# Where C's rows are folded, when a bias bank is seeded and when a doubled product is evacuated: one change to a gated state-space and MLP kernel on one core

## The chip, the core and the metric

The kernel runs on one core of a Trainium2 chip. The core has a matrix engine (TensorE, "PE" in the profile; its weight loads are "PEld"), a vector engine (VectorE, "DVE"), an activation engine (ScalarE, "ACT"), a general engine (GpSimd, "POOL") and a queue engine (SyncE, "SP"). Each takes its instructions strictly in the order in which the program wrote them, and waits on semaphores for what another engine has to finish first. SBUF is the working memory; PSUM, in eight banks, takes what PE computes. The metric is the device time of one launch in microseconds (us), as the median of several runs.

## What is computed

The input x is 2048 rows of 640 columns. Two branches are computed from it and mixed by a gate per row. Cut to what matters:

```python
g = sigmoid((x * gate_w).sum(-1))
# branch A: a diagonal complex state space, 640 states
Lam_bar = exp(exp(log_dt) * Lam)
Bu = x @ (((Lam_bar - 1) / Lam)[:, None] * Bmat).T
h_t = Lam_bar * h_{t-1} + Bu_t                       # over the 2048 rows
a = 2 * real(h @ Cmat.T) + x * Dskip
# branch B: an MLP, 640 -> 1728 -> 640
b = gelu_tanh(x @ w1 + b1) @ w2 + b2
out = g * a + (1 - g) * b
```

## The kernel before

The 2048 rows go through in four chunks of 512 (`c` = 0 to 3), and every chunk through four kinds of stage. The order of the stages is written out by hand at the end of the kernel (L911 to L951), chunk against chunk, so that one chunk's matmuls cover another's vector work.

- **State stage**, `ssm(c)` (L601). For each of five groups of 128 states (`ks`), PE makes x times B, real and imaginary, in two banks of ten matmuls in all (L610). ACT copies each bank out as `bu` (L613). DVE then turns the sequence into a real first-order recurrence, runs two scans (L556) and turns it back into `hs`: for each group `wa`, `wb`, `v`, two scans, `wa`, `wb`, `hs`. That takes DVE far longer than PE takes for the matmuls, so the chains of a chunk run on under the stages that follow. Between chunks the last column of the scan is carried by four small ACT instructions (L564).
- **GELU stage**, `ff1(c)` (L340). Thirteen banks (`kf` = 0 to 12) of five matmuls each (L300); ACT evacuates each by one GELU with its bias (L309). What is left over of the 1728 columns, 64 of them and the gate's one, is `last_tile` (L321): 20 small matmuls into a bank that ACT has seeded with the bias beforehand (`last_bank`, L317), with a GELU (L327) and a tanh for the gate (L329) behind them. In a dictionary `at` the stage is handed further work to issue ahead of a given `kf`.
- **Second MLP product**, `fin_b(c)` (L697). A two-by-two block product by seven multiplications instead of eight. Each multiplication is 2 times 7 matmuls of 320 columns (L708). Three of its names matter here. `X` is a pair of banks that collects several products; a `fork` (L720) is an ACT copy of that pair, halfway, into a new pair (`Y` or `Z`) on which other products are added. `Q` is the doubled product: it is needed in both column halves, so ACT evacuates it, scaled by the gate, into `gq` (`part_7`, L741), and a GpSimd DMA that adds on arrival (`twice`, `plus`, L653) brings it into both halves of a row tile. In chunks 0 to 2 the target of that DMA is the output's own tile `gb`; in chunk 3 (`gs` given) it is a tile of `GS`, two of which lie in the unused parts of `xA` and `w1c_lo`, and DVE adds them to `gb` later (L829).
- **Product with C**, `fin_a(c)` (L769): ten matmuls of 320 columns for each half of a row tile, on banks that ACT has seeded with x times Dskip (`seed`, L644); DVE adds gate and `gb` and the rows go out (L787). The last chunk has `fin_s` (L832) in its place, again by seven multiplications (L843, with DVE's evacuations at L860 and L872).

Before C can be used it has to be multiplied by complex factors: **`fold(ks)`** (L506). For each of the five groups of rows ACT writes two products into two f32 buffers `t1` and `t2` (L508 and L510, both in what is `xA`, free in that time), and DVE adds two more to them and writes C in place (L514, once for `CT_re`, once for `CT_im`). There is one `t1` and one `t2`. So the first DVE instruction of a fold waits for both ACT instructions (the second of them reads the old `CT_re`), and the ACT instructions of the next fold wait for the DVE instructions of this one. All five folds have to be through before `fin_a(0)`.

What sets the order on DVE is a planner with clocks of its own (L220 to L251). The pieces of a scan chain are put into a list with `later`. `dve_now(ready, cost, fn)` first lets out every piece of the list that could start ahead of `ready` on the planner's clock, and then issues `fn`. So the place of a fold on DVE is set by the planner's clock for ACT at the time that the fold is issued, while its place on ACT is simply where it stands in the program. `settle` lets out the carries in the same manner.

The PSUM banks go round: a tile that needs one gets the one that was given back first, in the order of the instructions that first write the tiles. On PE the stages around the change come in this order: `ff1(1)`, `ssm(1)`, `fin_b(0)`, `ff1(2)`, `fin_a(0)`; and at the end `fin_a(2)`, `fin_b(3)`, `fin_s(3)`.

Of the kernel before, what the change touches and what calls it, by code (L numbers as in the profile page):

```python
# [24 lines left out]
KF = (F + P - 1) // P  # L25
# [3 lines left out]
H = TPC // 2  # L29
# [13 lines left out]
def kernel(  # L43
# [32 lines left out]
    def bank(dtype=F32):  # L76
        return ps.tile([P, CH * 4 // (4 if dtype == F32 else 2)], dtype, name="bank")
# [153 lines left out]
    def let_out(until, chunk=-1):  # L231
        while pend:
            ready, cost, fn, _ = pend[0]
            start = max(ck.dve, ready)
            if start >= until and not any(x[3] == chunk for x in pend if chunk >= 0):
                return
            pend.pop(0)
            fn()
            ck.dve = start + cost

    def dve_now(ready, cost, fn):
        let_out(ready)
        fn()
        ck.dve = max(ck.dve, ready) + cost
# [4 lines left out]
    def act(cost):  # L249
        ck.act = max(ck.act, ck.pe + 0.2) + cost  # L250
        return ck.act  # L251
# [45 lines left out]
    def ff1_mm(p, c, kf, kd, t0=0, t1=CH, first=None, last=KD - 1):  # L297
        w, f0 = (w1a, 0) if kf < FA else (w1b, FA) if kf < FB else (w1c, FB)
        w = w[kd][:, (kf - f0) * P:(kf - f0 + 1) * P]
        nc.tensor.matmul(p[:, t0:t1], lhsT=w, rhs=xT[c][:, kd, t0:t1],  # L300
                         start=(kd == 0) if first is None else first, stop=(kd == last), skip_group_check=first is not None)
        pe(t1 - t0)

    def ff1_act(p, c, kf):
        s = kf if kf < FA else kf + 1 if kf < 2 * FA else FA
        for p0, p1 in ((0, RE), (RE, P)) if s == FA else ((0, P),):
            dst = eL[p0:p1, :] if p0 else gel[c][p0:p1, :, s, :]
            src = p[p0:p1, :] if p0 else p[p0:p1, :].rearrange("p (i t) -> p i t", i=2)
            nc.scalar.activation(out=dst, in_=src, func=ACT.Gelu_apprx_tanh, bias=b1_c[p0:p1, kf:kf + 1])  # L309
            act(0.69)  # L310
# [3 lines left out]
    def last_bank(c):  # L314
        p = bank()
        pv = p[:, 0:TPC * NL].rearrange("p (a n) -> p a n", a=TPC)
        nc.scalar.activation(out=pv, in_=b1x[:].rearrange("p (o n) -> p o n", o=1).to_broadcast([P, TPC, NL]), func=ACT.Identity)  # L317
        act(0.4)
        return p, pv
# [20 lines left out]
    def ff1(c, k0=0, at={}):  # L340
        for kf in range(k0, KF - 1):
            if kf in at:
                at[kf]()
            p = bank()
            if kf == KF - 3:
                last = last_bank(c)
            for kd in range(KD):
                ff1_mm(p, c, kf, kd)
            ff1_act(p, c, kf)
            let_out(ck.pe)  # L350
            if c > 0:
                settle()
        last_tile(c, *last)
        let_out(ck.pe)
# [151 lines left out]
    def fold(ks):  # L506
        t1, t2 = ft[:, 0, :], ft[:, 1, :]
        nc.scalar.activation(out=t1, in_=CT_im[:, ks, :], func=ACT.Identity, scale=n2im[:, ks:ks + 1])  # L508
        act(0.82)
        nc.scalar.activation(out=t2, in_=CT_re[:, ks, :], func=ACT.Identity, scale=n2im[:, ks:ks + 1])  # L510
        ready = act(0.82)

        def f(CT, sc, t):
            nc.vector.scalar_tensor_tensor(out=CT[:, ks, :], in0=CT[:, ks, :], scalar=sc[:, ks:ks + 1], in1=t,  # L514
                                           op0=ALU.mult, op1=ALU.add)

        dve_now(ready, 0.8, lambda: f(CT_re, c2re, t1))
        dve_now(ready, 0.8, lambda: f(CT_im, n2re, t2))
# [82 lines left out]
    def ssm(c, at={}):  # L601
        hs[c] = hsp.tile([P, 2, 2, KS, HT], BF16, name="hs")
        for ks in range(KS):
            if ks in at:
                at[ks]()
            bu = work.tile([P, 2, CH], BF16, name="bu", bufs=8)
            for ri, BT in enumerate((BT_re, BT_im)):
                p = bank()
                for kd in range(KD):
                    nc.tensor.matmul(p[:], lhsT=BT[ks >= KSA][:, kd, (ks % KSA if ks < KSA else ks - KSA) * P:][:, 0:P], rhs=xT[c][:, kd, :],  # L610
                                     start=(kd == 0), stop=(kd == KD - 1))
                    pe(CH)
                nc.scalar.activation(out=bu[:, ri, :], in_=p[:], func=ACT.Identity)  # L613
                act(0.6)
            scan_ops(c, ks, bu, ck.act)
            let_out(ck.pe)
            settle()
# [22 lines left out]
    def seed(ti):  # L640
        seeded[ti] = []
        for d0, d1 in cuts(ti):
            p = bank()
            nc.scalar.activation(out=p[:, 0:d1 - d0], in_=xn[ti][:, d0:d1], func=ACT.Identity)  # L644
            act(0.45)
            seeded[ti].append(p)
        if ti % TPC < TPC - 2:
            skip(ti + 2)
        if ti + TPC < NT - H:
            load_xn(ti + TPC)  # L650
# [43 lines left out]
    def twice(dst, src):  # L694
        plus(dst.rearrange("p (h d) -> p h d", h=2), src[:].rearrange("p (o d) -> p o d", o=1).to_broadcast([P, 2, HD]))

    def fin_b(c, at={}, gs=None):  # L697
        (a, b), (s1, d) = blocks(c)
        W = lambda h, k: w2_sb[:, h, k * KH:(k + 1) * KH, :]
        quad = [{} for _ in range(H)]  # L700
        gq = [None] * H

        def product(j, name, lhs, rhs, fresh):
            if name not in quad[j]:
                quad[j][name] = bank()
            p = quad[j][name]
            for s in range(KH):
                nc.tensor.matmul(p[:, 0:HD], lhsT=lhs[:, s, j * P:(j + 1) * P], rhs=rhs[:, s, :],  # L708
                                 start=fresh and s == 0, stop=s == KH - 1, skip_group_check=True)
                pe(HD)  # L710
            let_out(ck.pe)

        def both(name, lhs, rhs, fresh=False):
            for j in range(H):
                product(j, name, lhs, rhs, fresh)

        def fork(src, dst):
            for j in range(H):
                quad[j][dst] = bank()
                nc.scalar.activation(out=quad[j][dst][:, 0:HD], in_=quad[j][src][:, 0:HD], func=ACT.Identity)  # L720
                act(0.45)

        def out_of(name, half, h):
            for j in range(H):
                ti = c * TPC + half * H + j
                if gbs[ti] is None:
                    gbs[ti] = fwork.tile([P, D], F32, name="gb")
                nc.scalar.activation(out=gbs[ti][:, h * HD:(h + 1) * HD], in_=quad[j][name][:, 0:HD], func=ACT.Identity,  # L728
                                     scale=gcol[:, 1, ti:ti + 1])
                act(0.47)  # L730

        def hook(i):
            settle()
            if i in at:
                at[i]()

        def part_7():
            for j in range(H):
                ti = c * TPC + H + j
                gq[j] = fwork.tile([P, HD], F32, name="gq", bufs=2)  # L740
                nc.scalar.activation(out=gq[j][:], in_=quad[j]["Q"][:, 0:HD], func=ACT.Identity, scale=gcol[:, 2, ti:ti + 1])  # L741
                act(0.53)

        hook(0)
        both("X", a, W(0, 0), True)
        fork("X", "Y")
        both("Y", b, W(0, 1))
        out_of("Y", 0, 0)
        plus(flat(b), flat(N2[:]))
        hook(1)  # L750
        both("Q", N3, W(1, 0), True)
        both("X", N2, TB)
        fork("X", "Z")
        part_7()
        for j in range(H if gs else 0):
            twice(gs[H + j], gq[j])
        both("X", s1, TA)
        out_of("X", 1, 1)
        hook(2)
        both("Z", d, TC)  # L760
        out_of("Z", 1, 0)
        for j in range(0 if gs else H):
            twice(gbs[c * TPC + H + j][:], gq[j])
        hook(3)
        both("X", b, W(1, 1))
        out_of("X", 0, 1)
        settle()
# [133 lines left out]
    def skips(c, a=0):  # L901
        skip(c * TPC + a)
        skip(c * TPC + a + 1)
# [11 lines left out]
               5: lambda: (w_minus(1), w_plus(B12, TB)),  # L915
               9: lambda: (first_sums(), w_plus(TB, TA), w_plus(TC, TB))})
    gates(0)
    ssm(1)
    gates(1)
    load_xT(2)  # L920
    load_skip()
    fin_b(0, {1: lambda: fold(0), 2: lambda: fold(1), 3: lambda: fold(2)})
    gel_tile(2)
    ff1(2, 0, {1: lambda: fold(3), 4: lambda: fold(4), 7: lambda: skips(0), 9: lambda: seed(0), 11: lambda: seed(1)})
    gates(2)
    fin_a(0, sums(1))
    load_xT(3)
# [54 lines left out]
```

## Time and profile before

| | |
|---|---|
| median of 3 runs | 211.88 us (211.61 to 211.9) |
| the profiled execution | 211.5 us, of which the profiled span is 209.7 us |
| PE busy | 202.4 us, 97% of the span |
| DVE busy | 187.7 us, 89% |
| ACT busy | 147.1 us, 70% |
| POOL busy | 52.1 us, 25% |
| TensorE clock granted | 1.00 throughout |

Every instruction of the profile has a start and a duration in microseconds from the span's start, the engine, the line of the kernel, what it writes and reads, and in square brackets the idle time of its engine just ahead of it with the instruction that ended it. A group is marked by a count (x5). Matmuls are pipelined: the profile gives a single one of 512 columns 0.38 us, but they follow one another every 0.216 us (five start at 79.66, the next five at 80.74 us), and those of 320 columns every 0.136 us (five start at 86.50, the next five at 87.18 us). Short instructions of one kind follow one another on ACT sooner than the sum of their durations too, since the next begins before the last has fully ended.

Where the stages of interest lie on PE (from the timeline):

| stage | PE, from to |
|---|---|
| `ff1(1)` | 30.4 to 45.8 us |
| `ssm(1)` | 45.8 to 56.6 us |
| `fin_b(0)` | 56.6 to 69.9 us |
| `ff1(2)` | 69.9 to 86.5 us |
| `fin_a(0)` to `fin_a(2)` | 86.5 to 182.0 us |
| `fin_b(3)` | 182.0 to 195.3 us |
| `fin_s(3)` | 195.3 to 206.4 us |

### The profile page before, as it was taken

The numbers are of one execution on the slowest core, as the hardware profiler recorded it, in microseconds if no ns is written. First come the engines' busy times: TensorE is split into PE (matmuls) and PEld (weight loads), VectorE is DVE, ScalarE is ACT, GpSimd is POOL, SyncE is SP. The second block draws the span as 40 slices with busy tenths as digits, with TensorE's granted clock in tenths as the row PEclk, the third lists the DMA queues.
The fourth block names the chain that finished last, engine by engine and source line by source line (L and its number), as shares of the span: only waits on it lengthen the run. The fifth ranks groups of instructions, "written<-read, shape, count | busy, mean of one in ns | idle before, by whom it ended". The sixth has DMA issues, their size and how long they took to land.

```text
span 209.7 us, 3618 instructions
## 1 busy us (share of the span) xinstructions
PE 202.4 (97%) x1311; PEld 120.9 (58%) x1311; DVE 187.7 (89%) x308; ACT 147.1 (70%) x293; POOL 52.1 (25%) x83
## 2 busy tenths in 40 slices
PE   8999999989999997999999999999999999999982
PEld 5745444444577543576457777544447777777761
DVE  2589999999998899599999999999999999999583
ACT  3699989996768799991764895367987593058600
POOL 8344077314310500031001044100412045014000
PEclk9999999999999999999999999999999999999999
DMA  6999799999998330259933389920586969945403
GB/s 187 243 220 218 152 299 240 217 210 171 155 173 177 63 65 0 63 102 237 193 81 56 67 144 204 255 84 0 68 175 115 148 166 189 226 114 92 80 16 109
DMA packets 45126, 30.28 MB, mean 144 GB/s; under 512 B 26834, under 2 KB 42548, under 8 KB 45108
## 3 DMA queue, kind: packets, MB, share of 16 engines
q0 software_dynamic: 6448, 12.53, 35.3%
q1 hardware_dynamic: 38084, 17.03, 34.3%
q10 hardware_dynamic: 576, 0.49, 0.7%
q8 instruction: 10, 0.16, 0.3%
q14 instruction: 8, 0.07, 0.1%
HBM read 7.79 MB, written 2.62 MB: 50 GB/s over the span
## 4 chain that ended last, share of the span: by engine, by line
PE 74%; ACT 12%; DVE 6%; issue 3%; DMA 3%; POOL 0%; DVEq 0%
PE bank L610 21%; PE bank L708 18%; PE bank L782 16%; PE bank L300 15%; ACT gel L309 5%; DMA w1c_lo<-gq 3%; PE bank L324 1%; PE bank L259 1%; PE bank L843 1%; DVE ot L860 1%; DVE g L556 1%; ACT xA L508 1%; ACT TB L658 1%; DVE gb L872 1%; ACT xA L510 1%
## 5 line engine op out<-in xcount | busy, mean ns | idle before, releaser
L556 DVE TENSOR_TENSOR_SCAN g<-r_c,carry,v 128x512 bf16<-128x512 f32 x30 | 37.2, 1271 | 0.8
L613 ACT ACTIVATE bu<-bank 128x512 bf16<-128x512 f32 x40 | 23.2, 595 | 20.4 <-PE bank L610 20.4
L309 ACT ACTIVATE gel<-bank,colB 128x512 bf16<-128x512 f32 (+1 forms) x52 | 32.6, 696 | 1.6 <-PE bank L300 1.5
L708 PEld LDWEIGHTS <-gel 128*128 128x128 bf16 x280 | 27.3, 98 | 10.9
L782 PEld LDWEIGHTS <-hs 128*128 128x128 bf16 x240 | 23.4, 98 | 9.0
L708 PE MATMUL bank<-w_sb,gel 128*128 128x320 bf16 x168 | 24.1, 299 | 0.0
L300 PEld LDWEIGHTS <-w1a_sb 128*128 128x128 bf16 x162 | 14.2, 100 | 11.9
L782 PE MATMUL bank<-CT_re,hs 128*128 128x320 bf16 x120 | 20.2, 299 | 0.0
L782 PE MATMUL bank<-CT_im,hs 128*128 128x320 bf16 x120 | 20.2, 299 | 0.0
L728 ACT ACTIVATE gb<-bank,gcol 128x320 f32<-128x320 f32 x32 | 16.0, 525 | 5.4 <-PE bank L708 5.2
L720 ACT ACTIVATE bank<-bank 128x320 f32<-128x320 f32 x16 | 6.8, 424 | 17.1 <-PE bank L708 17.1
L610 PEld LDWEIGHTS <-BT_im 128*128 128x128 bf16 x100 | 9.8, 98 | 11.8
L610 PEld LDWEIGHTS <-BT_re 128*128 128x128 bf16 x100 | 9.6, 98 | 11.0
L534 DVE TENSOR_TENSOR v<-wa,wb 128x1024 bf16<-128x1024 bf16 (+1 forms) x25 | 14.2, 585 | 0.6
L534 DVE TENSOR_TENSOR wa<-TCOS,bu 128x1024 bf16<-128x1024 bf16 x20 | 13.7, 687 | 0.6
L300 PE MATMUL bank<-xA,w1a_sb 128*128 128x128 bf16 (+2 forms) x102 | 14.2, 296 | 0.0
L534 DVE TENSOR_TENSOR wa<-TCOS,g 128x1024 bf16<-128x1024 bf16 x20 | 13.8, 689 | 0.4
L534 DVE TENSOR_TENSOR wb<-TSIN,g 128x1024 bf16<-128x1024 bf16 x20 | 13.7, 684 | 0.0
L534 DVE TENSOR_TENSOR wb<-TSIN,bu 128x1024 bf16<-128x1024 bf16 x20 | 13.7, 684 | 0.0
L708 PEld LDWEIGHTS <-N 128*128 128x128 bf16 x112 | 11.0, 98 | 4.3
L300 PE MATMUL bank<-xB,w1a_sb 128*128 128x512 bf16 x60 | 13.3, 379 | 0.0
L300 PEld LDWEIGHTS <-w1b_sb 128*128 128x128 bf16 x80 | 7.8, 98 | 9.4
(182 smaller groups left out, 389.6 us busy)
## 6 DMA issues: line engine op xcount, KB each, us to landing
out_dram<-ot SPq DMA_DIRECT2D x15, 160.0 KB, 3.9
w_sb<-in_B_w_dram SPq DMA_DIRECT2D x4, 480.0 KB, 6.6
gb<-gq POOLq DMA_DIRECT2D x6, 320.0 KB, 5.2
gel<-N POOLq DMA_DIRECT2D x4, 448.0 KB, 5.4
xn<-in_A_x_dram SPq DMA_DIRECT2D x10, 160.0 KB, 3.4
N<-gel POOLq DMA_DIRECT2D x3, 448.0 KB, 4.5
gel<-gel POOLq DMA_DIRECT2D x3, 448.0 KB, 7.0
N<-N POOLq DMA_DIRECT2D x3, 448.0 KB, 7.9
```

The source lines that it names most:

```text
L259: nc.tensor.matmul(pA[:, 0:n], lhsT=ones(P), rhs=ones(n), start=True, stop=True)
L300: nc.tensor.matmul(p[:, t0:t1], lhsT=w, rhs=xT[c][:, kd, t0:t1], start=(kd == 0) if first is None else first, stop=(kd == last), skip_grou ...
L309: nc.scalar.activation(out=dst, in_=src, func=ACT.Gelu_apprx_tanh, bias=b1_c[p0:p1, kf:kf + 1])
L324: nc.tensor.matmul(p[:, a * NL:(a + 1) * NL], lhsT=xT[c][:, kd, a * P:(a + 1) * P], rhs=w1c[kd][:, n1c - NL:n1c], start=False, stop=(kd == ...
L534: nc.vector.tensor_tensor(out=o, in0=a, in1=b, op=op)
L556: nc.vector.tensor_tensor_scan(s["g"][:, ri, :], r_c[:, ks:ks + 1].to_broadcast([P, CH]), s["v"][:, ri, :], init, ALU.mult, ALU.add)
L610: nc.tensor.matmul(p[:], lhsT=BT[ks >= KSA][:, kd, (ks % KSA if ks < KSA else ks - KSA) * P:][:, 0:P], rhs=xT[c][:, kd, :], start=(kd == 0 ...
L613: nc.scalar.activation(out=bu[:, ri, :], in_=p[:], func=ACT.Identity)
L708: nc.tensor.matmul(p[:, 0:HD], lhsT=lhs[:, s, j * P:(j + 1) * P], rhs=rhs[:, s, :], start=fresh and s == 0, stop=s == KH - 1, skip_group_c ...
L720: nc.scalar.activation(out=quad[j][dst][:, 0:HD], in_=quad[j][src][:, 0:HD], func=ACT.Identity)
L728: nc.scalar.activation(out=gbs[ti][:, h * HD:(h + 1) * HD], in_=quad[j][name][:, 0:HD], func=ACT.Identity, scale=gcol[:, 1, ti:ti + 1])
L782: nc.tensor.matmul(p[:, 0:d1 - d0], lhsT=hs[c][:, a // H, j // KS, j % KS, (a % H) * P:][:, 0:P], rhs=CT[:, j % KS, d0:d1], start=False, s ...
```

## The change

Three edits. The first moves `last_bank` from ahead of the GELU bank 11 to ahead of bank 9 in the stages of chunks 1 to 3, and allocates it before that bank; with chunk 0 it stays at 11. The second, in `fin_b` of the last chunk alone, puts `part_7` and its two DMAs ahead of the product that ends in the second fork. The third moves the five folds: 0 and 1 go from hooks 1 and 2 of `fin_b(0)` into `ssm(1)`, ahead of its groups 3 and 4; 2, 3 and 4 take hooks 1, 2 and 3 of `fin_b(0)`; `ff1(2)`, which had folds 3 and 4, has none.

```diff
@@ ff1
         for kf in range(k0, KF - 1):
             if kf in at:
                 at[kf]()
+            if kf == (KF - 5 if c > 0 else KF - 3):
+                last = last_bank(c)
             p = bank()
-            if kf == KF - 3:
-                last = last_bank(c)
             for kd in range(KD):
                 ff1_mm(p, c, kf, kd)
@@ fin_b
         both("Q", N3, W(1, 0), True)
+        if gs:
+            part_7()
+            for j in range(H):
+                twice(gs[H + j], gq[j])
         both("X", N2, TB)
         fork("X", "Z")
-        part_7()
-        for j in range(H if gs else 0):
-            twice(gs[H + j], gq[j])
+        if not gs:
+            part_7()
         both("X", s1, TA)
@@ order of the stages
     gates(0)
-    ssm(1)
+    ssm(1, {3: lambda: fold(0), 4: lambda: fold(1)})
     gates(1)
     load_xT(2)
     load_skip()
-    fin_b(0, {1: lambda: fold(0), 2: lambda: fold(1), 3: lambda: fold(2)})
+    fin_b(0, {1: lambda: fold(2), 2: lambda: fold(3), 3: lambda: fold(4)})
     gel_tile(2)
-    ff1(2, 0, {1: lambda: fold(3), 4: lambda: fold(4), 7: lambda: skips(0), 9: lambda: seed(0), 11: lambda: seed(1)})
+    ff1(2, 0, {7: lambda: skips(0), 9: lambda: seed(0), 11: lambda: seed(1)})
```

## The prediction

> **What bounds the kernel now.** I read the page first: PE is busy 202.4 of 209.7 us at a granted clock of 1.00, and the chain that ended last gives PE 74% and ACT 12%. So a change can win only where PE stands still. The second view, the waits of PE, lists every stop:
>
> ```profile
> PE bank L843 <- DVE ot L860: 1.2, 2, 0.6
> PE bank L300 <- ACT gel L309: 1.1, 1, 1.1
> PE bank L324 <- ACT bank L317: 1.0, 2, 0.6
> ```
>
> Third, PE's timeline says when:
>
> ```profile
> 44.00 0.59 PE L300 MATMUL bank<-xB,w1c_hi 128*128 128x512 bf16 x2
> 45.24 0.25 PE L324 MATMUL bank<-w1c_lo,xB 128*128 128x65 bf16 x3 [0.64 <-ACT bank L317]
> ...
> 83.03 0.81 PE L300 MATMUL bank<-xB,w1c_lo 128*128 128x512 bf16 x3 [1.05 <-ACT gel L309]
> ...
> 85.90 0.25 PE L324 MATMUL bank<-w1c_lo,xB 128*128 128x65 bf16 x3 [0.33 <-ACT bank L317]
> ```
>
> Brackets count idle time after a modelled end; the loss is the start less the spacing of what ran before. At 45.24: 44.00 + 2 x 0.216 = 44.43, loss **0.81**. At 83.03: bank 10 began at 80.74, five matmuls take 1.08, loss **1.21**. Bank 12 began at 84.33 for 84.11: **0.22**. At 85.90: 84.33 + 1.08 = 85.41, **0.49**. In `fin_s` at 202.81: 200.69 + 10 x 0.136 = 202.05, **0.76**, and 0.74 more at the very end that no edit touches. The edits can get back at most 0.81 + 1.92 + 0.76 = 3.49.
>
> **Edit 1, bias bank.** In `ff1(1)` ACT works without a gap from 43.62 to 47.4; the seed (L317, 0.31 to the next start) stands behind GELU 10. Two GELUs earlier it is done by 44.0, before PE wants it. Gain 0.81: the last tile starts at 44.43, `ssm(1)` at 45.03. The GELUs swapped behind it gate nothing: the bank taken two allocations early shifts each to one whose GELU ended over 2 us before its reuse. In `ff1(3)` PE did not wait; nothing. In chunk 0 the ACT instruction already came ahead of bank 11's matmuls; nothing.
>
> **Edit 3, on ACT.** This is where part of it is given back.
>
> ```profile
> 54.08 1.19 ACT L613 ACTIVATE bu<-bank 128x512 bf16<-128x512 f32 x2
> 55.75 0.60 ACT L613 ACTIVATE bu<-bank 128x512 bf16<-128x512 f32 x1 [0.48 <-PE bank L610]
> 56.83 0.60 ACT L613 ACTIVATE bu<-bank 128x512 bf16<-128x512 f32 x1 [0.48 <-PE bank L610]
> 57.78 0.42 ACT L720 ACTIVATE bank<-bank 128x320 f32<-128x320 f32 x1 [0.35 <-PE bank L708]
> ...
> 61.99 0.81 ACT L508 ACTIVATE xA<-CT_im,n2im 128x640 f32<-128x640 bf16 x1
> 62.71 0.81 ACT L510 ACTIVATE xA<-CT_re,n2im 128x640 f32<-128x640 bf16 x1
> ```
>
> ACT is idle only 0.48 ahead of a `bu`, and fork Y at 57.78 has 0.33 to spare (done 58.20, PE's Y product starts 58.53). Four fold instructions at 0.72 (61.99 to 62.71) bring 2.88 into this stretch. Retimed with PE 0.81 earlier: last `bu` of group 2 at 51.70, the carry at 52.32 (0.94 long, as at 53.14 to 54.08), fold 0 at 53.26 and 53.98, group 3's `bu` at 54.70 and 55.18 (0.48 back to back).
>
> Fold 1 needs fold 0's buffers, hence DVE:
>
> ```profile
> 54.59 0.69 DVE L534 TENSOR_TENSOR wa<-TCOS,g 128x1024 bf16<-128x1024 bf16 x1
> ...
> 63.62 0.88 DVE L514 SCALAR_TENSOR_TENSOR CT_re<-CT_re,c2re,xA 128x640 bf16<-128x640 bf16 x1 [1.16 <-issue]
> 64.42 0.88 DVE L514 SCALAR_TENSOR_TENSOR CT_im<-CT_im,n2re,xA 128x640 bf16<-128x640 bf16 x1
> ```
>
> The first DVE half started 0.10 after the second ACT half ended (62.71 + 0.81). Its place in the new order I took from the planner's clock, for order alone: at group 3 ACT's clock stands at 50.92, plus 0.60 for a carry and 2 x 0.82 makes 53.16; the chain's second scan is due at 52.25 and goes first, its next `wa` at 53.46 and goes after. So fold 0 on DVE replaces the `wa` of 54.59. It starts at 53.98 + 0.81 + 0.10 = 54.90, the halves end at 55.78 and 56.58. Fold 1 on ACT: 55.83 and 56.63; group 4's `bu` 57.35 and 57.83; fork Y 58.31, done 58.73, and 0.06 later (lastbank's 45.18 to 45.24) PE starts Y at **58.79**. It was 58.53, and with the 0.81 it could have been 57.72. So a new wait of 1.07 appears and the 0.81 becomes a debt of **0.26**. No bank is late meanwhile: those that `ssm(1)` and `fin_b(0)` take were evacuated over 2 us before.
>
> What hides the rest in `fin_b(0)`: fold 2 takes fold 0's place on ACT (62.25, fork Z at 63.75 as PE allows), fold 3 follows the X evacuations at 67.03, fold 4 starts at 69.66 behind fold 3 on DVE (68.75 to 69.63). The last X evacuations and a carry end at 73.05; there GELU 0 of `ff1(2)` starts (it was 73.74). No PE instruction needs those X banks before bank 6. xT's load stays ahead of need and the SP queue gets nothing new.
>
> **Edit 3, `ff1(2)`.** Before, ACT spent 4 x 0.72 and two short waits on folds 3 and 4 here, and never caught up with PE. After, at 0.57 a GELU it catches up by bank 3 (74.77) and follows PE: GELU 8 at 80.06 (PE starts 0.26 late at 70.20, nine banks of 1.08, 0.15 latency). Then carry 0.92, seed 0.72, bias bank 0.31, so GELU 9 starts 82.60 and ends 83.29. Bank 11 reuses bank 8's slot (free at 80.8, wanted at 82.1: no wait); bank 12 reuses bank 9's, wanted at 83.15, start 83.35: 0.20 left. Last tile at 84.43 for 85.90: **1.47 gained up to here**. DVE's skips for the seeds are through by 78.4. If ACT's carry waited longer, each 0.1 is a 0.1 of bank 12.
>
> **Nothing gives it back in between.** PE has no wait from 86.5 to 202. DVE is busy 109.05 of those 115.5 us, so it must move too: it waited 2.47 for the gate (L329, now 86.75 for 88.02), so it moves by 1.27 and lags PE by 0.2. Had it not moved at all, `fin_s` would feel 0.45 of it: time 210.2.
>
> **Edit 2.** The tail, all engines:
>
> ```profile
> 188.80 0.42 ACT L720 ACTIVATE bank<-bank 128x320 f32<-128x320 f32 x1 [0.89 <-PE bank L708]
> ...
> 190.09 0.94 ACT L741 ACTIVATE gq<-bank,gcol 128x320 f32<-128x320 f32 x2
> ...
> 190.91 1.20 POOL L653 DMA_DIRECT2D xA<-gq  x1 [3.84 <-ACT gq L741]
> ...
> 191.62 1.71 POOL L653 DMA_DIRECT2D w1c_lo<-gq  x1
> ...
> 198.16 0.82 DVE L829 TENSOR_TENSOR gb<-gb,w1c_lo 128x640 f32<-128x640 f32 x1 [2.07 <-DMA w1c_lo<-gq]
> ```
>
> ACT idles 0.89 ahead of the fork. Q is complete at 187.65 and the `gated` copies end their turn at 187.82; both `gq` fit into 187.82 to 188.70, so the fork stays at 188.80. DMA issue moves from 190.91 to 188.64, the second from 191.62 to 189.35, 2.27 earlier; on POOL's queue only the DMA of 186.21 is ahead, its traffic over by 190.0 in the DMA share, and traffic of these began 1.6 after issue. Landing 195.8 for 198.06. DVE then reaches its first product (L872) when its `gq` is there (197.94), not at 199.70. From there PE leads: Y j=1 out at 200.9, X j=0 evacuated 201.58 to 202.12, PE on at 202.18 for 202.81: **0.63 gained**, 0.13 left. DVE needs the landing by 197.4; so 1.6 of slack.
>
> One page of the Trainium skill speaks against moving it: "SBUF — State Buffer", section "Who interferes with whom", has descriptor writing of a GpSimd-issued DMA blocked while VectorE holds the shared port pair. VectorE runs L534 from 188.66 to 190.7. [...] The trace shows the old issues beside VectorE's L811 all the while, landing in 4.3 and 6.4, which is what I used.
>
> **Sum.** 211.5 - 1.47 - 0.63 = 209.4 for the profiled execution; the median of the runs is 0.4 above it, so **209.8**, or 1.0% less.
>
> **Rivals.** (a) *The fork's new wait does not come*, because ACT and DVE interleave better than retimed: no debt, and the whole 0.81 stays: 1.07 more, 208.7. For: fold 1 follows fold 0 by only 0.05 on DVE. Against: 2.88 us of new ACT work has no room. Chance 0.10. (b) *The tail gives nothing*: the DMA lands after 197.4 all the same (traffic beside the earlier one; range of such DMAs 3.9 to 10.0): 210.4. Chance 0.12. (c) *DVE does not move*: 210.2, within the forecast's own range. (d) *Slower*: ACT is in order, and behind fold 1 stand the `bu` of group 4 and fork Y. If fold 0's DVE half comes behind group 4's chain, as it did at 63.62, and not ahead of the `wa` of 54.59, ACT holds until about 61.1 and PE with it. That is 6.2 more at the fork: 209.8 + 6.2 = 216.0. It is slower than before from 2.1 of delay on. Against: the order above; DVE has nothing else to wait for. Milder forms (a fold half waits for one `wa`, `wb` pair, 1.2) give 211.0. Chance 0.10 for slower, 0.05 for a delay that just eats the gain. (e) *The edits do nothing*: only if banks, not ACT, held PE at 83.03; but bank 8's GELU ends at 82.98 and PE starts at 83.03.
>
> **Numbers.** Forecast with (c) 0.63, 209.2 to 210.3 for retiming errors of 0.5; (a) 0.10, (b) 0.12, the eaten gain 0.05, (d) 0.10. The range 208.6 to 211.0 holds (a), (b), the forecast and the milder form of (d). A difference under 0.2% is what a measurement of this kernel cannot tell from none: faster 0.85, same 0.05, slower 0.10.
>
> **What would show it.** The waits of PE should lose L300 and L324 but for some 0.2 and gain an L708 behind ACT's L720 of about 1.0 near 58; fold 0 on DVE at 54.9; last tile of `ff1(2)` at 84.4; `gq` ahead of the second fork; the L829 wait on the DMA gone; L843's first wait under 0.2. A later fork Y, or an L300 wait that stays, makes it wrong.

## The result, and the profile after

The changed kernel takes **210.05 us** by the median of 6 runs (209.46 to 210.55), the kernel before 211.94 (211.61 to 212.15, 6 runs). The ratio is 0.9911, with a 95% interval of 0.9892 to 0.993. The forecast was 209.8 with a range of 208.6 to 211.0. The profiled execution took 210.25 us with a span of 208.5. Four runs of the experiments below were slow (215.13 and 435.2 of folds_alone, 360.0 of p7_alone, 214.7 of the kernel before): they count in the medians given there but not in the ratios, and without them the medians are 211.69, 211.48 and 212.13.

The waits of PE come first again:

```profile
PE bank L708 <- ACT bank L720: 1.0, 1, 1.0
PE bank L259 <- PEq L969: 0.8, 1, 0.8
PE bank L846 <- DVE ot L863: 0.6, 1, 0.6
```

Both waits of the GELU stages (L300, L324) are gone, one of the two in the last stage is gone, and a new one of 1.0 has come: L708 behind ACT's fork. (Behind the edit in `fin_b` every line number is 3 higher: L846 is the L843 of before.) PE's timeline gives the places:

```profile
45.18 0.26 PE L324 MATMUL bank<-w1c_lo,xB 128*128 128x65 bf16 x3
...
59.62 2.06 PE L708 MATMUL bank<-w_sb,gel 128*128 128x320 bf16 x14 [0.97 <-ACT bank L720]
...
84.20 0.81 PE L300 MATMUL bank<-xB,w1c_lo 128*128 128x512 bf16 x3
...
85.28 0.26 PE L324 MATMUL bank<-w1c_lo,xB 128*128 128x65 bf16 x3
...
201.56 1.52 PE L846 MATMUL bank<-CT_im,xA 128*128 128x320 bf16 x10
```

These times can't be set beside those of before as they stand. The same instructions, in the same order and far ahead of every edit, already differ. The state stage of chunk 0 begins on PE so, in the kernel before and then in the changed one:

```profile
19.61 1.24 PE L610 MATMUL bank<-xA,BT_re 128*128 128x512 bf16 x5
```

```profile
20.36 1.25 PE L610 MATMUL bank<-xA,BT_re 128*128 128x512 bf16 x5
```

The 0.75 was lost while the first loads of x and w1 came in: PE's matmul at L407 started at 6.83 before and at 7.58 after, and from there to L610 both took 12.78. So I compare **the stretch**: from that first L610 matmul to the first matmul of the last product X of `fin_s(3)` (202.81 before, 201.56 after). It is 202.81 - 19.61 = 183.20 before and 201.56 - 20.36 = **181.20** after: 2.00 less, where the prediction had 1.47 + 0.63 = 2.10. The two spans differ by only 1.2, because the profiled execution of before had the earlier start.

### The profile page after: what moved, and what is told of

Its sections match the earlier page's. It is cut to its first block, busy times and chain, and to the rows that moved or that the text cites. A ratio compares the mean times of both kernels' runs of the same rounds, so it can differ in the third digit from the quotient of the medians.

```text
span 208.5 us, 3622 instructions
## 1 busy us (share of the span) xinstructions
PE 202.8 (97%) x1311; PEld 121.2 (58%) x1311; DVE 188.1 (90%) x308; ACT 147.2 (71%) x293; POOL 51.9 (25%) x83
## 4 chain that ended last, share of the span: by engine, by line
PE 71%; DVE 17%; ACT 7%; issue 1%; POOL 1%; DVEq 0%
PE bank L708 25%; PE bank L785 16%; PE bank L300 13%; PE bank L610 10%; PE bank L846 5%; DVE g L556 3%; ACT gel L309 3%; DVE wa L534 2%; DVE wb L534 2%; DVE g L472 1%; PE bank L259 1%; DVE v L534 1%; DVE TSIN L473 1%; DVE TCOS L473 1%; DVE N L688 1%
## 5 line engine op out<-in xcount | busy, mean ns | idle before, releaser
L708 PEld LDWEIGHTS <-gel 128*128 128x128 bf16 x280 | 27.3, 98 | 12.0 <-issue 1.2
L708 PE MATMUL bank<-w_sb,gel 128*128 128x320 bf16 x168 | 24.3, 299 | 1.0 <-ACT bank L720 1.0
L300 PEld LDWEIGHTS <-w1a_sb 128*128 128x128 bf16 x162 | 14.6, 102 | 11.9
L610 PEld LDWEIGHTS <-BT_im 128*128 128x128 bf16 x100 | 9.8, 98 | 11.8
L610 PEld LDWEIGHTS <-BT_re 128*128 128x128 bf16 x100 | 9.6, 98 | 11.0
L534 DVE TENSOR_TENSOR v<-wa,wb 128x1024 bf16<-128x1024 bf16 (+1 forms) x25 | 14.2, 585 | 0.6
L300 PE MATMUL bank<-xA,w1a_sb 128*128 128x128 bf16 (+2 forms) x102 | 14.7, 302 | 0.0
L534 DVE TENSOR_TENSOR wa<-TCOS,bu 128x1024 bf16<-128x1024 bf16 x20 | 13.7, 687 | 0.6
L534 DVE TENSOR_TENSOR wa<-TCOS,g 128x1024 bf16<-128x1024 bf16 x20 | 13.8, 689 | 0.4
L534 DVE TENSOR_TENSOR wb<-TSIN,bu 128x1024 bf16<-128x1024 bf16 x20 | 13.7, 685 | 0.0
L534 DVE TENSOR_TENSOR wb<-TSIN,g 128x1024 bf16<-128x1024 bf16 x20 | 13.7, 685 | 0.0
L708 PEld LDWEIGHTS <-N 128*128 128x128 bf16 x112 | 11.0, 98 | 4.3
L300 PEld LDWEIGHTS <-w1b_sb 128*128 128x128 bf16 x80 | 7.8, 98 | 9.4
L300 PE MATMUL bank<-xB,w1a_sb 128*128 128x512 bf16 x60 | 13.3, 379 | 0.0
```

The source lines that it names most:

```text
L534: nc.vector.tensor_tensor(out=o, in0=a, in1=b, op=op)
```

## The experiments

The kernels ran in three groups, each on one chip beside the kernel before: its median was 212.14 in the first group (bank_alone to spread_2_4, 31 runs), 211.91 in the second (after_again to spread_split) and 212.06 in the third (the last four; 11 runs each). "Stretch" is the one above, from each kernel's own profile.

| kernel | median, us | ratio to before (95%) | first L610 | stretch | less than before |
|---|---|---|---|---|---|
| bank_alone | 210.96 | 0.9949 (0.9932 to 0.9967) | 20.51 | 182.11 | 1.09 |
| folds_alone | 211.84 | 0.9985 (0.9962 to 1.0008) | 20.03 | 182.76 | 0.44 |
| p7_alone | 211.49 | 0.9968 (0.9949 to 0.9987) | 20.23 | 182.55 | 0.65 |
| spread_2_4 | 209.91 | 0.9903 (0.9871 to 0.9936) | 20.50 | 180.70 | 2.50 |
| after_again | 210.25 | 0.9907 (0.9884 to 0.993) | 20.39 | 181.20 | 2.00 |
| spread_again | 209.10 | 0.9864 (0.9843 to 0.9884) | 19.38 | 181.11 | 2.09 |
| spread_seed8 | 208.94 | 0.9857 (0.9836 to 0.9878) | 20.27 | 179.85 | 3.35 |
| spread_split | 207.61 | 0.9796 (0.9775 to 0.9818) | 19.49 | 179.85 | 3.35 |
| after_third | 210.53 | 0.9927 (0.9902 to 0.9952) | 20.23 | 181.78 | 1.42 |
| split_alone | 210.18 | 0.9915 (0.989 to 0.994) | 20.35 | 182.68 | 0.52 |
| seed8_again | 208.55 | 0.9851 (0.9828 to 0.9875) | 19.68 | 179.85 | 3.35 |
| split_again | 209.32 | 0.9858 (0.9835 to 0.9881) | 19.38 | 181.92 | 1.28 |

**bank_alone**: the kernel before with the bias bank's edit.

```diff
-            p = bank()
-            if kf == KF - 3:
+            if kf == (KF - 5 if c > 0 else KF - 3):
                 last = last_bank(c)
+            p = bank()
```

> Only the bias bank moves; folds and doubled product as before. Theory (three separate PE stops, each with its own price): the last tile of the second GELU stage starts at once (0.81 gained) and nothing eats it, since no fold stands ahead of fork Y; in the third GELU stage the wait on the bias bank (0.49) goes, but GELU 9 comes 0.31 later and with it bank 12; the 1.21 ahead of bank 11 stays. Sum 0.81 + 0.49 - 0.31 = 0.99 less, about 210.9. Rival (the bias bank is worth nothing by itself, ACT has the same work before and after): within 0.2 of 211.9. Startup: if the 0.75 by which PE began its second GELU stage later in the changed kernel's profile (31.15 for 30.41) is chance, it need not be here.

The last tile of `ff1(1)` starts without a gap, as wanted, and the median came at 210.96. In `ff1(2)` the wait for the bias bank turned into a second wait for a GELU, beside the one that was there, since ACT still has folds 3 and 4 to do in that stage (in folds_alone, where they are elsewhere, no wait for a GELU is left):

```profile
83.12 0.81 PE L300 MATMUL bank<-xB,w1c_lo 128*128 128x512 bf16 x3 [0.90 <-ACT gel L309]
...
84.72 0.81 PE L300 MATMUL bank<-xB,w1c_lo 128*128 128x512 bf16 x3 [0.36 <-ACT gel L309]
```

Up to the last tile of `ff1(2)` the edit is worth 1.00 (85.80 - 20.51 against 85.90 - 19.61): 0.81 of it in `ff1(1)`, and only 0.19 here. The theory had 0.99.

**folds_alone**: the kernel before with the three lines of the folds.

```diff
-    ssm(1)
+    ssm(1, {3: lambda: fold(0), 4: lambda: fold(1)})
-    fin_b(0, {1: lambda: fold(0), 2: lambda: fold(1), 3: lambda: fold(2)})
+    fin_b(0, {1: lambda: fold(2), 2: lambda: fold(3), 3: lambda: fold(4)})
-    ff1(2, 0, {1: lambda: fold(3), 4: lambda: fold(4), 7: lambda: skips(0), 9: lambda: seed(0), 11: lambda: seed(1)})
+    ff1(2, 0, {7: lambda: skips(0), 9: lambda: seed(0), 11: lambda: seed(1)})
```

> Only the folds move; bias bank and doubled product as before. Theory: the 0.81 ahead of the last tile of the second GELU stage stays, fork Y is late and PE loses about 1.07 in front of Y; in the third GELU stage PE's waits (1.92 in all) go. Sum 1.92 - 1.07 = 0.86 less, about 211.05. Rival (the folds in the state stage are hidden, so the new wait came with the bias bank's earlier PE): 1.9 less, about 210.0.

The theory (0.86 less) was missed. The median is 211.84 and the interval holds 1. Its profile has the fork's wait without the 0.81 that pays for most of it, and this wait in `ff1(2)`, which I had not summed:

```profile
85.91 0.25 PE L324 MATMUL bank<-w1c_lo,xB 128*128 128x65 bf16 x3 [0.24 <-ACT bank L317]
```

The matmuls ahead of it began at 84.43, so 85.51 was due and 0.40 is lost: with the old place of the seed L317 stands behind both seeds and the GELU between, and is late even without folds on ACT. Product Y starts 1.12 later than before, counted from L610 (60.07 - 20.03 against 58.53 - 19.61), and 1.53 is won in `ff1(2)`. So this edit is worth 0.41 up to the last tile, and the median can't tell that from none. The rival, 1.9 less, is out: the fork waits here too, without the bias bank's edit.

**p7_alone**: the kernel before with `part_7` and its two DMAs ahead of the product X of the second fork, in chunk 3.

```diff
+        if gs:
+            part_7()
+            for j in range(H):
+                twice(gs[H + j], gq[j])
         both("X", N2, TB)
         fork("X", "Z")
-        part_7()
-        for j in range(H if gs else 0):
-            twice(gs[H + j], gq[j])
+        if not gs:
+            part_7()
```

> Only the doubled product's evacuation moves, in the last chunk. Theory: 0.63 less at the first wait of the last product with C (0.76 falls to 0.13), about 211.3, and the profile is the same as before up to the last chunk. Rival (the DMA's landing is hidden by something else that ends as late): within 0.2 of 211.9.

The median came at 211.49 and the stretch at 0.65 less; PE's wait of 0.60 ahead of product X is gone. The stretch of before is known from one profile only, but its two parts come again where an edit leaves them alone: 66.27 for 66.29 up to the last tile of `ff1(2)` here (86.50 - 20.23), and 116.88 for 116.91 behind it in folds_alone (202.79 - 85.91). Added up to the last tile of `ff1(2)`, the first two edits alone are worth 1.00 + 0.41 = 1.41, and together 1.37: they add. In the tail they don't quite: the three alone save 0.09, 0.03 and 0.63 there, together also 0.63, and 0.12 of the wait stays (201.56 for 200.08 + 10 x 0.136 = 201.44).

**spread_2_4** and **spread_again**: the changed kernel with fold 0 one group earlier, so that ACT has two groups between the folds.

```diff
-    ssm(1, {3: lambda: fold(0), 4: lambda: fold(1)})
+    ssm(1, {2: lambda: fold(0), 4: lambda: fold(1)})
```

> The changed kernel with fold 0 one group earlier (ahead of group 2 of the second state stage), so that the 2.88 us of fold work on ACT lie over three groups. Theory (ACT is only short of room behind group 3; from the second bu on it has 1.7 us of idle time ahead of fork Y that two folds so placed can use): fork Y starts within 0.3 of when X is ready, PE's wait before Y falls from 0.97 to under 0.3, and the 0.7 to 1.1 go through to the end: 209.0 to 209.3 where the changed kernel has 210.05. Rival (the sum of ACT's work up to fork Y is what counts, wherever it stands): wait and time as in the changed kernel, 210.05.

> The first fold is one group earlier (group 2 in place of 3), the second stays at group 4. Theory: the fork's wait of 0.97 us goes, and the time is that of the changed kernel less 0.97 if the weights w2 are there in time: 209.0 to 209.3 us; in the profile no wait of L708 on L720, and none of L324 near 46. Rival (the late w2 load of the last profile belongs to this order of the work, not to chance): the load's wait of about 0.9 on ACT is there again, L324 waits about 0.5 near 46, and the time is 209.6 to 210.0 us. Second rival (ACT's added 2.88 us of folds count wherever they stand): 210.0 to 210.3 us, as the changed kernel.

The fork's wait is gone in both profiles. But in both, ACT's copy of w2 waited for its load, and its queue carried that delay to the bias bank: in spread_again (ACT, then PE)

```profile
36.51 2.07 ACT L658 ACTIVATE TA<-w_sb 128x2240 bf16<-128x2240 bf16 x1 [1.28 <-DMA w_sb<-in_B_w_dram]
```

```profile
45.25 0.25 PE L324 MATMUL bank<-w1c_lo,xB 128*128 128x65 bf16 x3 [0.88 <-ACT bank L317]
```

That is 45.25 for 43.77 + 0.43 = 44.20, a loss of 1.05; in spread_2_4 it is 0.64. Without it the stretches would be 181.11 - 1.05 = 180.06 and 180.70 - 0.64 = 180.06: 1.14 less than the changed kernel's, which is all that the fork had cost. The load is far ahead of the fold, so the two orders are the same up to there. By the median the theory (209.0 to 209.3) held in spread_again, at 209.10, and not in spread_2_4, at 209.91. In both profiles the late load is there, which spread_again's rival had named; its time of 209.6 to 210.0 did not come.

**spread_seed8** and **seed8_again**: that, and the first seed one bank earlier.

```diff
-    ff1(2, 0, {7: lambda: skips(0), 9: lambda: seed(0), 11: lambda: seed(1)})
+    ff1(2, 0, {7: lambda: skips(0), 8: lambda: seed(0), 11: lambda: seed(1)})
```

> As the last one, and the first seed one GELU earlier, so that the carry, the seed and the bias bank no longer stand in one row ahead of GELU 9. Theory (bank 12's 0.22 us of lateness is ACT's row of 0.92 + 0.72 + 0.31): bank 12 is on time, and the time is 0.2 us less than that of the last kernel. Rival (the row only moves, and bank 11 is late instead): no difference, within 0.1 us.

> Folds at groups 2 and 4, first seed at bank 8, tail as in the changed kernel. Theory: 1.35 us less than the changed kernel between the first L610 matmul and product X of the last tile (179.85 us), so 208.7 to 208.95 us by the median. Rival (w2's load comes late in this order, as in the two profiles of the order without the earlier seed): ACT waits 0.9 to 1.3 for w_sb near 37, L324 waits near 45, and the median is 209.2 or more.

Bank 12 is on time, and both profiles give the stretch of 179.85: 181.20 - 1.14 - 0.21. No load was late in either. The medians are 208.94 and 208.55, the second 0.15 below what was expected. Beside spread_again (209.10) in the same group, the runs can't show a gain of 0.2.

**after_again** and **after_third**: the changed kernel as it is, in the second and third group.

> The changed kernel once more, beside the kernels that go further. Theory (PE's stops alone make the time; what differs ahead of the state stage is chance of the first loads): 210.0 to 210.3 us, some 0.9% under the kernel before, and from the first L610 matmul of the trace to the start of the product X of the last tile (1.36 us of wait less than before at fork Y, the two GELU waits, the bias bank) 181.2 us, as in the run that is already known. Rival (part of the gain is itself chance of one execution): the stretch from the first L610 to that product differs by more than 0.2 us from 181.20.

> The changed kernel, third look, beside three kernels with the tail's last product split or not. Theory: 210.0 to 210.3 us; 181.2 us from the first L610 matmul to the start of the last tile's product X. Rival (starts of up to 0.9 us earlier or later decide the median): a median that differs by 0.4 or more from 210.15 while the stretch of 181.2 us stays.

The first gave the stretch of 181.20 again, to the hundredth, and a median inside what was expected. The second gave 210.53 and a stretch of 181.78, which neither side of the expectation had: 0.56 of the 0.58 is a stop of PE that is not in the other two profiles (below).

**spread_split**, **split_alone** and **split_again**: the last piece of product Z (columns 192 to 320) in a bank of its own, so that PE need not wait for DVE's evacuation of the first piece: with folds at 2 and 4 and the seed at 8 (the first and third), or alone on the changed kernel.

```diff
-            fork(j, Z)
+            fork(j, Z, LAST if j == H - 1 else ((0, HD),))
...
-            done(Z, j, 1, 0, *cols[-1])
+            done(Z, j, 1, 0, *cols[-1], len(cols) - 1)
```

> As the last one, and the last piece of product Z (columns 192 to 320) in a bank of its own, so that PE does not wait for VectorE's evacuation of the first piece (0.74 us lost by PE at the very end in the kernel before, 0.6 by the brackets). One fork of 0.42 on ACT becomes two shorter ones. Theory (PE's end sets the last evacuation): 0.45 us less than the last kernel, since the last evacuation and its store still follow. Rival (VectorE's two evacuations and the stores behind them are the end whatever PE does): under 0.15 us, or up to 0.2 more for the second fork.

> The changed kernel with nothing but the last piece of product Z in a bank of its own. Theory (in the profile of the kernel with all the steps, the last evacuation ended 0.60 us sooner after the first L610 matmul, and the rest of the 1.33 us between the medians was an earlier start): 0.5 to 0.65 us less than the changed kernel of this call, 209.5 to 209.7. Rival (the split itself is worth the 1.33): 208.7 to 208.9.

> As the last one with the split product. Theory (the split is worth 0.5 to 0.65, the rest of the earlier 1.33 was chance of the start): 208.1 to 208.4 us. Rival (1.33 is what the split does): 207.4 to 207.7 us.

DVE's last evacuation in the changed kernel, then in spread_split:

```profile
205.23 0.35 DVE L863 SCALAR_TENSOR_TENSOR ot<-bank,gcol,gb 128x128 bf16<-128x128 f32 x1 [0.53 <-PE bank L846]
```

```profile
200.95 1.81 DVE L866 SCALAR_TENSOR_TENSOR ot<-bank,gcol,gb 128x320 bf16<-128x320 f32 x4 [0.18 <-PE bank L847]
```

From the start of the last product X to the end of that evacuation the changed kernel takes 4.02 (201.56 to 205.23 + 0.35), and all three kernels with the split 3.42 (199.34 to 200.95 + 1.81 in spread_split): the split is worth **0.60** in every profile, where the first expectation had 0.45. The medians said 1.33 (208.94 to 207.61), then 0.35 (210.53 to 210.18), then 0.77 the other way (208.55 to 209.32), and none of the three medians fell where the theory or the rival had it. The profiles show what lay between in the third group. split_again, PE and ACT:

```profile
59.58 2.06 PE L708 MATMUL bank<-w_sb,gel 128*128 128x320 bf16 x14 [1.56 <-ACT bank L720]
```

```profile
52.40 0.83 ACT L508 ACTIVATE xA<-CT_im,n2im 128x640 f32<-128x640 bf16 x1 [2.13 <-DMA CT_im<-in_A_C_im_dram]
```

C's load landed at 52.3, so the early fold 0 waited 2.13 for it, the `bu` behind it stood still, and the fork was late again. Y starts at 59.58 for 55.95 + 1.90 = 57.85: 1.73 lost. With 0.35 for a w2 load that was late here too (44.55 for 44.20 at L324), 179.85 + 2.08 = 181.93, and 181.92 is measured. The expectation (208.1 to 208.4) had no term for that. In split_alone a GpSimd DMA landed 8.6 after issue, not 5.8 as in the changed kernel's profile:

```profile
70.58 2.08 PE L708 MATMUL bank<-w_sb,gel 128*128 128x320 bf16 x14 [1.13 <-DMA gel<-N]
```

It began 10.97 after product Y, not 9.51 (69.13 - 59.62): 1.46 lost, and 182.68 - 1.46 = 181.22. In after_third the same DMA took 7.7 and cost 0.56: 181.78 - 0.56 = 181.22. So the stretch of every kernel built on the changed one is 181.20 with the stops that its profile shows on PE added or taken off, to within 0.03.

## Why the prediction was right, and what it left out

The prediction's times are those of the profile before. So from each number of the changed kernel's profile the 0.75 of its later start is taken off first.

- **Bias bank.** The last tile of `ff1(1)` was forecast at 44.43; 45.18 - 0.75 = 44.43. That is confirmed, here and by bank_alone.
- **The retiming of `ssm(1)`.** ACT and DVE of the changed kernel:

```profile
54.03 0.81 ACT L508 ACTIVATE xA<-CT_im,n2im 128x640 f32<-128x640 bf16 x1
...
56.59 0.83 ACT L508 ACTIVATE xA<-CT_im,n2im 128x640 f32<-128x640 bf16 x1
57.44 0.83 ACT L510 ACTIVATE xA<-CT_re,n2im 128x640 f32<-128x640 bf16 x1
58.18 1.07 ACT L613 ACTIVATE bu<-bank 128x512 bf16<-128x512 f32 x2
59.13 0.76 ACT L720 ACTIVATE bank<-bank 128x320 f32<-128x320 f32 x2
```

```profile
55.66 0.88 DVE L514 SCALAR_TENSOR_TENSOR CT_re<-CT_re,c2re,xA 128x640 bf16<-128x640 bf16 x1 [0.35 <-issue]
56.47 0.88 DVE L514 SCALAR_TENSOR_TENSOR CT_im<-CT_im,n2re,xA 128x640 bf16<-128x640 bf16 x1
57.26 0.69 DVE L534 TENSOR_TENSOR wa<-TCOS,g 128x1024 bf16<-128x1024 bf16 x1
```

  Fold 0 on ACT at 53.28 (forecast 53.26), on DVE at 54.91 (54.90) and ahead of the `wa`, fold 1 at 55.84 (55.83). Its second half starts 0.09 after DVE's second half ends (56.47 + 0.88 = 57.35, 57.44), not 0.05, so it is at 56.69 for 56.63; with the `bu` the fork is at 58.38 (58.31) and PE starts Y at 58.87 (58.79). The debt at the fork is 0.34, not 0.26.
- **`ff1(2)`.** Bank 12 starts at 84.20 for 83.55 + 2 x 0.216 = 83.98: 0.22 lost (0.20). The last tile is at 84.53 (84.43). The 0.10 of difference is the fork's 0.08 and bank 12's 0.02.
- **DVE follows.** The gate's L624 stood at 88.22 before, and after the change it is

```profile
87.80 0.17 DVE L624 TENSOR_SCALAR gcol<-gz 128x4 f32<-128x4 f32 x1 [2.20 <-ACT gz L329]
```

  or 87.05 with the 0.75 off: it moved by 1.17 (forecast 1.27), and nothing is given back up to the tail. Rival (c) is out.
- **The tail.** The changed kernel's queues, ACT, POOL and DVE:

```profile
187.20 0.93 ACT L741 ACTIVATE gq<-bank,gcol 128x320 f32<-128x320 f32 x2
188.19 0.42 ACT L720 ACTIVATE bank<-bank 128x320 f32<-128x320 f32 x1
```

```profile
188.01 1.20 POOL L653 DMA_DIRECT2D xA<-gq  x1 [1.55 <-ACT gq L741]
188.72 1.71 POOL L653 DMA_DIRECT2D w1c_lo<-gq  x1
```

```profile
194.44 0.82 DVE L832 TENSOR_TENSOR gb<-gb,xA 128x640 f32<-128x640 f32 x1
195.17 0.82 DVE L832 TENSOR_TENSOR gb<-gb,w1c_lo 128x640 f32<-128x640 f32 x1
```

  Both `gq` stand ahead of the fork, the fork is no later for it, and DVE adds without a wait. From the last tile of `ff1(2)` to product X it is 201.56 - 85.28 = 116.28 for 116.91: 0.63 less, as forecast, and rival (b) is out. The DMAs landed 4.0 and 5.1 after issue, at 192.0 and 193.8. Nothing held them up: VectorE ran L534 from 188.25 to 190.27 beside both issues, POOL's two instructions took 1.20 and 1.71 as before, and they landed sooner than the 4.3 and 6.4 of before. The prediction read the page of the Trainium skill wrongly here: the same section ("SBUF — State Buffer", "Who interferes with whom") says of `tensor_tensor` that it was not seen to stall such a DMA, and L534 and L811 both are TENSOR_TENSOR. What a VectorE operation that holds the shared pair would cost, no run here shows.
- **Rivals (a), (d) and (e).** All three are out: the fork did wait (a), fold 0's DVE half did come ahead of the `wa` (d), and the GELU waits did go (e).

**What the sum left out.** The mechanism held, and the terms of the sum to 0.10: 2.00 in the stretch for 2.10. The median is 0.25 above the forecast. Of that, 0.10 is the terms, and 0.04 is the kernel before, at 211.94 for the 211.9 from which the forecast went down (211.5 and the 0.4 between that execution and the median). The 0.11 left is the 1.89 between the medians for the 2.00 of the stretch. The other two groups have 1.66 and 1.53 between the medians, and pooled (18 runs) the changed kernel takes 210.27, 0.47 above the forecast and still inside its range. These 18 runs go from 209.46 to 211.27, about as wide as the change is large. One cause is in a profile: in after_third a DMA landed late and cost 0.56, and the sum had no term for that. That late landings make up all of what is missing isn't shown.

The prediction also never looked at C's load when it moved a fold to 53.3. In the trace of before it landed at 38.4 + 9.5 = 47.9, so 5 us were to spare; the later runs show landings from 46.9 to 52.3. By estimate fold 0 at group 3 would be clear of the latest by 0.7 (53.28, less 0.23 for the earlier start of that execution, against 52.3). That it is clear was luck, as far as the prediction goes. At group 2 fold 0 gains 1.14 over the changed kernel when the load is on time. With the load at 52.3 PE lost 1.73 ahead of Y, which is 0.59 more than the 1.14 that the changed kernel loses there.

**The best version seen** has the folds at 2 and 4 and the seed at 8 (0.9857 and 0.9851 in two groups), with the split of the last product 0.9796 and 0.9858. That the split helps by more than the scatter is shown by the profiles, not by the medians.

**Open.** Whether fold 0 at group 2 has anything to do with the late loads. They were late in three of the six profiles with it and in none of the other eight; but the programs are alike up to there, and what the three have in common is another thing: PE reached L407 at 6.60, 6.51 and 6.60, earlier than in all the rest (6.71 to 7.73). Where the first loads were quickest, w2 and C came late. Part of the way from w2 to C can be seen. In these three, SP waited 2.0 to 2.4 at L206 for a load of w2 to land, and 1.1 to 1.6 in the other eleven. C's loads stand behind L206 on the same queue, and the second was issued at 40.2 to 41.2 instead of 38.3 to 39.3; in split_again the first half of C also took 5.07 to issue, for 3.2 to 3.5 in the rest. Why w2 is late where the start is quick isn't shown.

## What to carry to other kernels

Retiming in-order queues by hand, from the durations and spacings of one trace, gave the starts that the sum rests on to 0.1 us: as long as nothing else is the limit, a stop of PE is simply added to what follows. Before two executions are compared, subtract what they already differ by ahead of the first edit, and compare a stretch that both have in common. When work is moved earlier, look up when its loads landed, and how far that varies: three microseconds of slack are no cover where a landing moves by five.

## What the runs showed of the hardware

- PE reached its first L610 between 19.38 and 20.51 us in fourteen profiles of programs that are alike up to there. Nearly all of the difference arises in the first 8 us, while the first loads come in (spread_2_4 lost another 1.1 later, 0.95 of it as a wait for a w1 load).
- C's second load, a DMA that transposes, was issued between 38.3 and 41.2 and landed 8.6 to 11.1 later. The GpSimd DMA `gel<-N` of `fin_b(0)` landed 4.8 to 8.6 after issue; PE waited for it in the two profiles with 7.7 and 8.6, and in none of the twelve with at most 6.1.
